# A memory-attention and FFT kernel: full-array products that may run as four 32-column tiles, a score unit of four groups, a new order

## The chip, the cores and the metric

The kernel runs on one core of a Trainium2 chip. The core's engines run side by side, each with an instruction queue of its own: TensorE (PE, matrix products into PSUM), VectorE (DVE), ScalarE (ACT), GpSimd (POOL), and SyncE (SP), which here only issues transfers. The metric is the device time of one execution in microseconds. The kernel before was timed three times: 245.85 us median, 242.32 lowest, 248.95 highest.

## The reference

Two branches over the same sequence length and width (2,048 tokens, 640 features) are mixed by a gate per token:

```python
x = A_x
g = sigmoid((x * gate_w).sum(-1, keepdims=True))
return g * A(x, wq, wk, wv, wo, beta) + (1 - g) * B(B_x, B_w_r, B_w_i)

def A(x, ...):                       # 32 heads of 20, 4 segments of 512 tokens
    for s in range(4):
        p = softmax(qs @ ks^T * scale + mask)      # causal inside the segment
        a_dot = p @ vs
        a_mem = (phi(qs) @ M) / (phi(qs) @ z + 1e-6)   # phi(t) = t + 1 if t > 0 else exp(t)
        o = sigmoid(beta) * a_mem + (1 - sigmoid(beta)) * a_dot
        M += phi(ks)^T @ vs;  z += sum(phi(ks))
    return o @ wo

def B(x, w_r, w_i):
    return irfft2(rfft2(x) * (w_r + 1j * w_i))
```

## The kernel before, in words

**The work.** Each of four segments has the projections of queries, keys and values (`proj_direct`, `proj_tile`, `v_part`), the feature map phi of queries and keys (in `proj_tile`: an exponential on ScalarE, a maximum and a minimum on VectorE, per tile of 128 rows by 512 tokens), the read of the memory built by earlier segments (`mem_read_tile`), the scores and their exponentials (`qk_unit`), causal masks on GpSimd (`mask`), the values (`pv_flipped` in segments 0 to 2, `pv_group` in segment 3), and the update of the memory (`mem_update`). The FFT branch (`fft`) is a chain of products with constant tables, named in the profile by their operands: `fcat,xsb` and `big,Ac` first, `Bt,tt` and `tt,Yt` in the middle, `big,Cp` last. `finish_tile` adds both branches and writes the result. Ten products on zeros (`warm_up`) run on TensorE while the first inputs are loaded.

**Shapes of TensorE.** `mms` (line 506) issues a group of products. It has a `mode`: 0 is the full array, weights of 128 rows by 128 columns; 1 is the score shape, weights of 20 rows by 64 columns, eight side by side; 2 is the split shape, weights of 128 rows by 32 columns, four side by side, each of which writes 32 PSUM partitions. A product with mode -1 may run full or, as four split products of 32 weight columns, in mode 2. Only the output projections of segments 0 to 2 (`finish_tile`, `oproj`, traced on line 520) have -1. The projections, the FFT, the memory's read and update and the gate's transposition have mode 0, and so have the value products of segment 3. Values of segments 0 to 2, the value projection of odd token tiles and the gated FFT products (`G,fbg`) have mode 2.

**Scores.** A head group is four heads; a segment has eight groups. `UNITS` (line 582) lists a pair's five score units: (first group, key blocks a), (first, b), (second, a), (both, last blocks c), (second, b). Each unit takes all four PSUM banks of the pool `qk`, then one exponential by ScalarE (two for b in the last segment) writes the tile `ex`. `ex` has three slots of 5,120 elements per partition, and group g uses slot g mod 3 (counted through all segments); a group's values are read from its slot before the third group behind it overwrites it.

**The order.** What runs when is no loop order. `record` lists all operations with what they read and write; `ORDER` (line 587) is a written list of 2,328 entries, each the number of an operation and which of its possible engines runs it. `Sched.schedule` walks the list with a model of costs (`HOPS`, `COST`, `QUEUE`) to place PSUM banks, semaphores and, for mode -1, the shape; `emit` writes each engine's instructions in that order with the waits that the reads and writes ask for. An engine carries out its instructions strictly in that order. All transfers but a few at the start and the end are on SP's queue.

For mode -1 the shape is chosen in `schedule`: a product that adds to a bank keeps the shape that the bank was begun in; one that begins a bank takes the shape of the product ahead of it; and behind a score unit it takes that of the next fixed work, or the full array where that is a score unit again.

**The gate.** The gate weight is the 641st column of `wv`; the value projection's second part has 321 columns and gives the gate's sums with it (`v_part`). In odd token tiles, whose rows are written in another order by split products, two exponentials of 64 rows bring them back; in even tiles it is one of 128 rows.

## Time and profile before

| | |
|---|---|
| median of three runs | 245.85 us |
| the profiled execution's own time | 246.08 us |
| its span, first to last instruction | 244.0 us |
| granted TensorE clock, mean | 0.993 |
| busy: TensorE / VectorE / ScalarE / GpSimd | 226.9 / 200.7 / 200.4 / 167.2 us |
| TensorE products / weight loads | 4,349 / 4,361 |
| transfers | 42.17 MB, 173 GB/s on average |

Busy time is the union of an engine's instructions as the profile draws them. Products of TensorE overlap in it: one of 320 columns is drawn about 300 ns long although the next can start some 136 ns later, so distances between starts say more than lengths. In the shape of a group, "128*32 128x320" means weights of 128 rows by 32 columns and a moving operand of 128 rows by 320 columns. Most products are issued by one line (L522 of `mms`; L520 for those that are split), so they are told apart by the names of their operands. A few records of products are missing in the trace.

### The profile page before, as it was taken

How to read it: one execution, taken by the hardware profiler on the slowest of the kernel's cores; microseconds unless marked ns; L12 is line 12 of the kernel's file. 1: busy time of each engine (PE TensorE's matmuls, PEld its weight loads, DVE VectorE, ACT ScalarE, POOL GpSimd, SP SyncE). 2: the span in 40 equal slices, each digit the busy share in tenths (PEclk: the TensorE clock that was granted, in tenths of full speed). 3: DMA queues.
4: the chain of work that ended last, by engine and by line, in shares of the span. 5: the costliest groups of instructions: out<-in, count | busy, mean ns of one | idle time of the engine just before them, and what ended most of it. 6: DMA issues, size and time to landing. Idle time of an engine off the chain costs nothing.

```text
span 244.0 us, 10261 instructions
## 1 busy us (share of the span) xinstructions
PE 226.9 (93%) x4349; PEld 140.8 (58%) x4361; DVE 200.7 (82%) x478; ACT 200.4 (82%) x243; POOL 167.2 (69%) x298
## 2 busy tenths in 40 slices
PE   7999999999979999899799979998999989999994
PEld 2674666766455665455575545565554546566793
DVE  0299989889999987999997998998999996735473
ACT  2388989988989999899898879999999968687801
POOL 8334069447959938649779895968898783857730
PEclk9999999999999999999999999999999999799999
DMA  7999959996977975849637583463876759382213
GB/s 168 301 330 268 209 173 182 233 194 199 214 209 131 189 222 147 183 141 252 159 98 203 134 247 97 126 169 105 227 172 201 182 130 206 95 87 83 72 67 108
DMA packets 58928, 42.17 MB, mean 173 GB/s; under 512 B 30020, under 2 KB 55172, under 8 KB 58884
## 3 DMA queue, kind: packets, MB, share of 16 engines
q1 hardware_dynamic: 57188, 40.71, 67.9%
q10 hardware_dynamic: 1696, 0.82, 1.2%
q8 instruction: 34, 0.56, 1.0%
q14 instruction: 10, 0.08, 0.1%
HBM read 23.32 MB, written 12.30 MB: 146 GB/s over the span
## 4 chain that ended last, share of the span: by engine, by line
PE 63%; DVE 16%; ACT 10%; DMA 7%; issue 2%; ACTq 0%; SPq 0%; DVEq 0%
PE psum L522 57%; ACT ex L1271 8%; PE psum L520 5%; DMA r<-r_scr 2%; DMA xT<-in_A_x_dram 2%; DVE Yt L1452 2%; DVE Pt L1447 2%; DVE phk L1093 2%; DMA dnc<-u_scr 2%; DVE oU L1534 1%; DMA u_scr<-ub 1%; ACT et L1080 1%; DVE Cp L533 1%; DVE ub L533 1%; DVE G L1493 1%
## 5 line engine op out<-in xcount | busy, mean ns | idle before, releaser
L1271 ACT ACTIVATE ex<-psum 128x2048 bf16<-128x2048 f32 (+4 forms) x92 | 138.6, 1506 | 15.5 <-PE psum L522 13.1
L1292 POOL TENSOR_SCALAR_AFFINE_SELECT ex<-ex 128x256 bf16<-128x256 bf16 (+2 forms) x224 | 122.6, 570 | 35.3 <-ACT ex L1271 32.8
L522 PE MATMUL psum<-qkp 20*64 20x64 bf16 (+5 forms) x1280 | 32.7, 271 | 3.9 <-ACT ex L1271 2.9
L522 PE MATMUL psum<-xT,wk 128*128 128x256 bf16 (+1 forms) x280 | 33.8, 281 | 0.6 <-DMA xT<-in_A_x_dram 0.4
L522 PE MATMUL psum<-wv,xT 128*32 128x320 bf16 (+3 forms) x400 | 29.4, 301 | 0.0
L522 PE MATMUL psum<-xT,wq 128*128 128x512 bf16 (+1 forms) x123 | 28.0, 385 | 0.8 <-issue 0.5
L1447 DVE TENSOR_TENSOR Pt<-psum,Wt 128x642 bf16<-128x642 f32 x32 | 25.5, 821 | 0.6 <-PE psum L522 0.2
L522 PEld LDWEIGHTS psum<-qkp 20*64 20x64 bf16 x1280 | 13.4, 103 | 21.6 <-ACT ex L1271 15.1
L522 PEld LDWEIGHTS psum<-xT,wk 128*128 128x128 bf16 (+1 forms) x280 | 19.8, 99 | 8.3 <-issue 1.8
L520 PE MATMUL psum<-wo,oU 128*32 128x320 bf16 x480 | 22.2, 305 | 0.5 <-DVE oU L1542 0.2
L522 PE MATMUL psum<-big,Ac 128*128 128x161 bf16 (+2 forms) x96 | 17.6, 257 | 2.0 <-DVE va L1123 1.5
L522 PE MATMUL psum<-ex,va 128*32 128x64 bf16 (+3 forms) x576 | 17.6, 257 | 1.8 <-DVE Pt L1447 1.3
L522 PE MATMUL psum<-big,Cp 128*128 128x321 bf16 (+1 forms) x96 | 18.1, 307 | 1.0 <-DVE G L1493 0.6
L522 PEld LDWEIGHTS psum<-wv,xT 128*32 128x32 bf16 (+1 forms) x400 | 14.5, 96 | 7.4 <-issue 2.0
L1123 DVE TENSOR_TENSOR va<-psum,ebx 128x320 bf16<-128x320 f32 x32 | 15.3, 483 | 2.9 <-PE psum L522 1.8
L914 POOL TENSOR_TENSOR xsb<-xf 128x320 bf16<-128x320 bf16 (+2 forms) x9 | 7.6, 846 | 14.4 <-DVE xsb L914 10.3
L522 PEld LDWEIGHTS psum<-ex,va 128*32 128x32 bf16 x576 | 11.0, 96 | 10.7 <-DVE Pt L1447 2.2
L1493 DVE TENSOR_TENSOR G<-eo,psum 128x320 bf16<-128x320 f32 x32 | 14.9, 478 | 2.3 <-PE psum L522 1.9
L533 DVE CAST ot<-psum 128x320 bf16<-128x320 f32 x18 | 8.5, 488 | 9.8 <-PE psum L520 7.9
L1080 ACT ACTIVATE et<-qu 128x512 bf16<-128x512 bf16 x25 | 15.3, 625 | 0.9 <-DVE phk L1093 0.9
L522 PE MATMUL psum<-tt,Yt 128*128 128x256 bf16 (+1 forms) x96 | 15.6, 274 | 0.3 <-DVE mem L1165 0.2
L1452 POOL TENSOR_TENSOR Yt<-Pt 128x321 bf16<-128x321 bf16 x17 | 12.7, 758 | 4.4 <-PE psum L522 3.9
(96 smaller groups left out, 401.2 us busy)
## 6 DMA issues: line engine op xcount, KB each, us to landing
qkp<-qk_scr SPq DMA_DIRECT2D x28, 160.0 KB
tt<-tab_tt SPq DMA_DIRECT2D x8, 512.0 KB, 4.3
qk_scr<-qu SPq DMA_DIRECT2D x12, 256.0 KB, 3.0
u_scr<-ub SPq DMA_DIRECT2D x12, 256.0 KB, 3.1
xsb<-in_A_x_dram SPq DMA_DIRECT2D x8, 320.0 KB, 4.9
oU<-u_scr SPq DMA_DIRECT2D x15, 128.0 KB, 3.2
out_dram<-ot SPq DMA_DIRECT2D x12, 160.0 KB
Wt<-in_B_w_r_dram SPq DMA_DIRECT2D x16, 80.2 KB, 3.2
```

The lines of the kernel that those rows point to most:

```text
L520: h = e.matmul(dst, wt, r_, start=st, stop=sp_, **{**kw, "tile_position": (0, q), "skip_group_check": True})
L522: h = e.matmul(o_, l_, r_, start=st, stop=sp_, **kw)
L533: alts["dve"] = (lambda e: e.tensor_copy(dst(), src()), 67 + 1.04 * n, 68.0)
L914: self.either(lambda e, dst=dst, src=src, d0=d0, n=n, op=op: e.tensor_tensor(xs.ap(o + dst, [D, 2], [1, n]), xf.ap(src + d0, [321, 2], [1, ...
L1080: self.one("act", lambda e: e.activation(et.ap(0, [1, L]), qsl(), ACT.Exp), L, [qb], [b("et", pi_)], late, name="phi_exp")
L1093: fmin = lambda e: e.tensor_tensor(dst(), dst(), et.ap(0, [1, L]), ALU.min)
L1123: self.one("dve", lambda e: e.tensor_tensor(va.ap(i * H * VW + h0 * VW, [VW, nh], [1, DH]), self.ps(bank, 0, [DH, nh], [1, DH]), self.ebx. ...
L1271: self.one("act", lambda e, d=d, q=q: e.activation(self.ex.ap(*d), self.ps(bank, *q), ACT.Exp, scale=SC), n, [bank], [self.exb(s, 2 * pr + ...
L1292: self.one("pool", lambda e: e.affine_select(self.ex.ap(e0 + d0, [1280, 4], [1, n], np_=np_), self.ex.ap(e0 + s0, [1280, 4], [1, n], np_=np_),
L1447: self.one("dve", lambda e, ri=ri, Pt=Pt, Wt=Wt, wo_=wo_, bank=bank: e.tensor_tensor(Pt.ap(ri * 322, [644, 2], [1, KD]), self.ps(bank, 0, ...
L1452: fn = lambda e, r=r, a0=a0, a1=a1, op=op, Pt=Pt, Yt=Yt: e.tensor_tensor(Yt.ap(r * 322, [1, KD]), Pt.ap(a0 * 322, [1, KD]), Pt.ap(a1 * 322 ...
L1493: self.one("dve", lambda e, q=q, n2=n2, bank=bank, eo=eo: e.tensor_tensor(self.G.ap(n2 * D + 639 * q, [1 - 2 * q, 320]), eo.ap(q, [1, 320] ...
```

## The change

- **Shapes.** Every full-array product but those of the last segment's values and the warm-up gets mode -1 in place of 0. Its cost in the planner is a pair, one for each shape.
- **Score units.** In segments 0 to 2 the units are listed per half segment (`HALF`): the last key blocks of four groups are one unit with one exponential of 2,048 elements per partition, behind the units a and b of groups 0, 1, 2 and ahead of the values of group 0; units a and b of group 3 follow, then the values of groups 1, 2 and 3. These blocks go to the tails of four slots (`hole`), so `ex` has four slots; the main part of a group still uses one of three. The rest of the fourth slot houses small tiles (`ub`, `Mz`, `dn`, gate tiles, `beta`).
- **Feature map.** The two tiles that are stored together get one exponential, one maximum and one minimum of 1,024 in place of two each of 512.
- **Memory read.** One reciprocal of 32 for both halves of a token tile in place of two of 16.
- **Gate.** Odd token tiles get their sums from products of one column (`odd_gates`, ten per segment) and one exponential per segment.
- **Planner and buffers.** The planner's costs are new (hops per engine, a price for a second wait, a fixed 95 for a change of shape, costs per transfer), tiles are packed to 32 bytes, `gT` shares a place with `dnr` and `rs` lies on the first columns of `fcat`. `ORDER` is a new list, with 2,264 entries.

The core of the diff (the list `ORDER`, most of the planner and the tile addresses are left out):

```diff
+def pe_cost(cols, mode):
+    if mode == 0:
+        return round(sum(max(n / 2.4 + 2.6, 25.2) for n in cols)), 178 if cols[-1] > 60 else 161
+    if mode == 2:
+        return round(sum(max(n / 9.6 + 1.0, 7.5) for n in cols)), 203 if cols[-1] > 64 else 213
+    return {12: (265, 239), 16: (261, 212), 24: (155, 269), 48: (300, 262)}[len(cols)]
...
-            self.mms(items, [b("w" + which + "a"), b("w" + which + "b"), xb[c], bank], [], prio, name="proj", mode=0)
+            self.mms(items, [b("w" + which + "a"), b("w" + which + "b"), xb[c], bank], [], prio, name="proj", mode=-1)
...
-                    self.mms(items, [b("xsb", 2 * nb + l2 // 2), b("fcat"), bank], [], prio, name="F1", mode=0)
+                    self.mms(items, [b("xsb", 2 * nb + l2 // 2), b("fcatF"), bank], [], prio, name="F1", mode=-1)
...
-                    self.mms([(th, n)], [b("Ac", c, nb) for nb in range(4)] + [b("big"), bank], [], prio, name="D", mode=0)
+                    self.mms([(th, n)], [b("Ac", c, nb) for nb in range(4)] + [b("big"), bank], [], prio, name="D", mode=-1)
...
+    HALF = (((0,), 0), ((0,), 1), ((1,), 0), ((1,), 1), ((2,), 0), ((2,), 1), ((0, 1, 2, 3), 2), (0, -1), ((3,), 0), ((3,), 1), (1, -1), (2, -1), (3, -1))
     UNITS = (((0,), 0), ((0,), 1), ((1,), 0), ((0, 1), 2), ((1,), 1))
...
     def attend(self, s):
         b = self.b
-        for pr in range(4):
+        if s < 3:
+            for half in range(2):
+                for u, (gps, kind) in enumerate(self.HALF):
+                    if kind < 0:
+                        self.pv_flipped(s, 4 * half + gps)
+                    else:
+                        self.qk_unit(s, 4 * half, u, (gps, kind))
+        for pr in range(4) if s == 3 else ():
             for u, parts in enumerate(self.UNITS):
-                self.qk_unit(s, pr, u, parts)
+                self.qk_unit(s, 2 * pr, u, parts)
...
-            outs = [((e0 + sh, [1280, 4], [step, 2], [1, 128]), (0, [512, 4], [128, 2], [1, 128]))]
+            outs = [((sh, [1280, 4], [5120, 4], [1, 128]), (0, [512, 4], [128, 4], [1, 128]))]
...
+        if t not in (1, 2, 4) or not ((which == "q" and s >= 1) or (which == "k" and s <= 2)):
+            return
+        m = 1 if t == 2 else 2
+        first, n_el = t + 1 - m, m * L
...
+        self.one("act", lambda e: e.activation(et.ap(0, [1, n_el]), qt.ap(po, [1, n_el]), ACT.Exp), n_el, rb, ebuf, late, name="phi_exp")
...
+        self.one("dve", lambda e: e.reciprocal(dn.ap(32, [1, 32]), dn.ap(0, [1, 32])), 32, [b("dn", k, q) for q in range(2)], [rb], prio, fix=145, name="mem_rec")
...
+    def odd_gates(self, s, prio, xT, xb):
+        self.Sc.group += 1
+        b = self.b
+        bank = Bank(1, "gen")
+        for i in (1, 3):
+            items = []
+            for c in range(5):
+                items.append((lambda i=i, c=c: (self.ps(bank, i // 2, [1, 1]), xT.ap(c * L + i * P, [1, P]), self.wv.ap(c * (D + 1) + D, [1, 1]),
+                                                c == 0, c == 4, {"skip_group_check": True}), 1))
+            self.mms(items, [b("gw"), bank] + xb, [], prio, name="gatep", mode=-1)
+        self.one("act", lambda e: e.activation(self.gr.ap(4 * s + 1, [2, 2]), self.ps(bank, 0, [1, 2]), ACT.Exp, scale=-1.0), 2,
+                 [bank], [b("gr", s, 1)], prio, name="gate_exp")
```

## The prediction

> **What bounds the kernel now.** First the page: the span, the busy shares and the chain that ended last.

> ```profile
> span 244.0 us, 10261 instructions
> ...
> PE 226.9 (93%) x4349; PEld 140.8 (58%) x4361; DVE 200.7 (82%) x478; ACT 200.4 (82%) x243; POOL 167.2 (69%) x298
> ...
> PE 63%; DVE 16%; ACT 10%; DMA 7%; issue 2%; ACTq 0%; SPq 0%; DVEq 0%
> ```

> The path runs on TensorE for 63% of the span; VectorE and ScalarE carry most of the rest. Next, busy time by stretch, since an average hides stages (columns: stretch, its length, then busy us and instructions of PE, weight loads, DVE, ACT, POOL; then clock, DMA share, GB/s).

> ```profile
> 0.00:50.00 50.00, 48.23 (x724) 30.04 (x726) 37.01 (x94) 36.90 (x56) 25.97 (x42) 1.00 0.94 236
> 50.00:195.00 145.00, 135.10 (x2418) 80.20 (x2425) 134.29 (x314) 134.10 (x152) 113.14 (x210) 1.00 0.69 174
> 195.00:235.00 40.00, 37.98 (x1071) 25.41 (x1060) 25.32 (x64) 28.53 (x35) 28.13 (x47) 0.96 0.54 112
> ```

> Up to 50 us and from 195 us TensorE is alone at the limit (48.2 of 50, 38.0 of 40). Between them three engines stand within a microsecond of each other: 135.1, 134.3 and 134.1 of 145 us. So in the long middle an edit that lightens one engine only hands the bound to the next; it has to lighten all three.

> "Busy" does not say how much of TensorE's time is products. The timeline of PE does (start, length, operation; the shape is weights rows*columns, then the moving operand; counts merge neighbours). The distance between two starts is the real price.

> ```profile
> 29.14 0.84 PE L522 MATMUL psum<-wv,xT 128*128 128x320 bf16 x5
> 29.82 0.38 PE L522 MATMUL psum<-xT,wq 128*128 128x512 bf16 x1
> ...
> 30.58 0.39 PE L522 MATMUL psum<-fcat,xsb 128*128 128x128 bf16 x4
> 30.80 0.38 PE L522 MATMUL psum<-xT,wq 128*128 128x512 bf16 x1
> ...
> 45.48 0.72 PE L522 MATMUL psum<-ex,va 128*32 128x512 bf16 x24
> 46.03 0.72 PE L522 MATMUL psum<-wv,xT 128*32 128x321 bf16 x16
> ...
> 86.31 0.60 PE L522 MATMUL psum<-xT,wk 128*128 128x256 bf16 x4
> 86.84 0.73 PE L522 MATMUL psum<-ex,va 128*32 128x512 bf16 x24
> 87.40 0.86 PE L522 MATMUL psum<-wv,xT 128*32 128x320 bf16 x20
> 88.19 0.42 PE L522 MATMUL psum<-qkp 20*64 20x320 bf16 x16
> ```

> Five full-array products of 320 columns take 29.82 - 29.14 = 0.68 us, 0.136 each; four of 128 columns take 0.22, 0.055 each. The 24 tile products at 45.48 are six pieces of 512, 384, 192 and three times 64 columns, four tiles side by side: 1,280 columns, which at the full-array pace would take 4 x 0.136 = 0.54; they take 0.55. So **a split product streams as fast as a full one**, and going from one kind of work to another in the same shape costs nothing (87.40 - 86.84 = 0.56 again). Where the shape changes there is a gap: four products of 256 columns are 0.435, yet 0.53 passes to 86.84; five split products of 320 are 0.68, yet 0.79 passes to 88.19. That is 0.095 to 0.11 us **per change of shape**.

> **The change part by part.** (1) Shapes. Following the starts through the whole timeline, full and split meet directly 58 times (31 into split, 27 into full); in 46 of them the gap is under 0.115 us, so nothing but the change of shape is there (4.53 us in total, 0.0985 each). First and last of the 46:

> ```profile
> 6.99 0.39 PE L522 MATMUL psum<-G 128*128 128x512 bf16 x1
> 7.30 0.40 PE L522 MATMUL psum<-xT,wk 128*32 128x256 bf16 x8
> ...
> 234.75 0.62 PE L522 MATMUL psum<-fcat,on 128*128 128x128 bf16 x8
> 235.30 0.91 PE L522 MATMUL psum<-wo,oTl 128*32 128x320 bf16 x20
> ```

> After the change a full product takes the shape of what ran before it, or, behind a score unit, of the next fixed work. What stays fixed in the full shape is the warm-up and the value products of the last segment, which make six of the 46 (the first one above and five from 194 us on). So 40 changes go, 40 x 0.0985 = -3.9 us (bounds 0, if the new order lets none go, and -5.7 for all 58). In the 12 others TensorE waits for data anyway; I take nothing.

> (2) Score units. In three of four segments the last key blocks of four head groups share one unit instead of two: six units fewer, each entered and left by a change of shape, 12 x 0.095 = -1.1 us. The streamed columns are the same.

> (3) The gate column of the odd token tiles moves into 40 full products of one column. The nearest row are the last segment's products of 21 columns:

> ```profile
> 222.89 1.17 PE L522 MATMUL psum<-va,ex 128*128 128x21 bf16 x40
> 223.98 0.43 PE L522 MATMUL psum<-qkp 20*64 20x512 bf16 x12
> ```

> 40 in 1.09 us less one change of shape: 0.025 each, so +1.0 us. TensorE: -3.9 - 1.1 + 1.0 = **-4.0 us**.

> (4) ScalarE (groups by shape: count, busy us, mean ns, idle before).

> ```profile
> L1271 ACT ACTIVATE ex<-psum 128x2048 bf16<-128x2048 f32 x56 | 105.1, 1877 | 7.2 <-PE psum L522 5.5
> L1080 ACT ACTIVATE et<-qu 128x512 bf16<-128x512 bf16 x25 | 15.3, 625 | 0.9 <-DVE phk L1093 0.9
> L1271 ACT ACTIVATE ex<-psum 128x1024 bf16<-128x1024 f32 x12 | 12.3, 1024 | 1.7 <-PE psum L522 1.4
> L1121 ACT ACTIVATE gate<-psum 64x1 f32<-64x1 f32 x16 | 2.6, 165 | 0.5
> ```

> Twelve exponentials of 1,024 become six of 2,048: 12.3 to 6 x 1.877 = 11.3, -1.0. Of 30 feature exponentials of 512 (the 25 here and five on the first segment's buffer), 24 become 12 of 1,024; that size from memory is not in the trace: between 1.024 (the score row of that size) and 2 x 0.625. I take the first: 24 x 0.625 - 12 x 1.024 = -2.7 (other end 0). Sixteen gate exponentials become four: -12 x 0.165 = -2.0. ScalarE: **-5.7 us** (-3.0).

> (5) VectorE.

> ```profile
> L1093 DVE TENSOR_TENSOR phk<-phk,et 128x512 bf16<-128x512 bf16 x15 | 9.8, 655 | 0.0
> L1163 DVE RECIPROCAL dn<-dn 128x16 f32<-128x16 f32 x24 | 5.5, 241 | 0.3
> L1160 DVE SCALAR_TENSOR_TENSOR dn<-psum,ebg 128x16 f32<-128x16 f32 x24 | 3.5, 152 | 0.1
> L1219 DVE RECIPROCAL dnr<-dnc 128x128 f32<-128x128 bf16 x3 | 2.8, 945 | 0.4 <-DMA dnc<-u_scr 0.4
> ```

> 24 feature maxima and 24 minima (655 ns is the longest group) become 12 and 12. What goes is 24 times the fixed part of an instruction, at most the 152 ns of one on 16 elements and at least nothing; the middle, 0.08, gives -1.9. The 24 reciprocals of 16 become 12 of 32: the slope between the two rows is (945 - 241) / 112 = 6.3 ns, so 342 each, 5.8 to 4.1, -1.7. VectorE: **-3.6 us** (-1.7 to -5.3).

> The joint reciprocal adds a wait: the first half's multiplication now stands behind the second half's products, some three of 154 columns at 0.065, and VectorE's whole in-order queue behind it, with the PSUM copies that TensorE waits for. That is 0.2 us twelve times, 2.4 at worst; I take nothing, since another VectorE instruction can stand in between. A joint feature exponential starts one PSUM copy later, and so does the transposing transfer of the key features on SP's queue (their number is the same); the products that read them come microseconds later, so nothing, or 0.6 us for each of six pairs on ScalarE if that cover is gone. GpSimd's masks and SP's transfers keep their number. The smaller buffers (a tile shared by two uses, a table's columns reused in the last segment) wait for work long done: nothing, or a few tenths per segment.

> So all three bounding engines lose nearly the same: 4.0, 5.7, 3.6. The least relieved sets the pace: I take **-3.7 us** on the span.

> (6) The order. It is new for every engine, and the trace cannot price it; bounds come from what an order can move: TensorE's idle time from 50 to 235 us, 9.9 + 2.0 = 11.9 us. At best it goes, at worst it doubles. I take a quarter off, -3.0, because waits behind exponentials and VectorE shrink with (4) and (5).

> Sum: 246.1 us (the profiled execution, span 244.0 and 2.1 around it) - 6.7 = 239.4. That execution lies 0.2 above the median 245.85, so from the median it is 239.1: **239 us**.

> **The rivals.** *The order gives more.* Half or more of the 11.9 us go beside the 3.7: 229 to 235, say 233. For it: three engines at 93% have slack that a search can pair. Against it: each such wait needs another engine free at that place.

> *Balance kept, waits back.* The work goes but the new order's waits take it back, or few shapes are unified because score units sit between: 241 to 250, say 244. For it: three engines bound together, so a gain needs all three at each place.

> *Slower: the four-group unit starves ScalarE.* There are still three slots for score tiles. The fourth group's exponential overwrites the first group's slot, so it waits for that group's values, which wait for the joint unit's masks.

> ```profile
> L1292 POOL TENSOR_SCALAR_AFFINE_SELECT ex<-ex 128x256 bf16<-128x256 bf16 x128 | 60.1, 480 | 29.7 <-ACT ex L1271 28.4
> L1292 POOL TENSOR_SCALAR_AFFINE_SELECT ex<-ex 64x512 bf16<-64x512 bf16 x64 | 43.4, 683 | 5.3 <-ACT ex L1271 4.4
> ```

> Masks 2 x 0.480 + 0.683, then the value products 0.73 (row at 86.84): 2.4 us without a score exponential, six times, 14 us. Behind the waiting instruction stands ScalarE's whole in-order queue, and behind that the PSUM copies TensorE needs. Before, the joint unit of two came with one more unit behind it as cover. Against it: of ScalarE's 200.4 us the rows of part 4 hold 117.4 of score exponentials, so up to 83 are other work (less by the last segment's smaller ones) that can be placed there. It decides when more than 11.6 of the 14 us stay unfilled (6.7 gained plus 4.9 for 2%); with all of it unfilled the time is 239 + 14 = 253.

> *Split products are starved of weights.* A split product needs four weight loads and four products. If each pair kept the 0.025 us of the row at 222.89, a split product could not be under 0.10 us. That touches 296 products of 88 to 176 columns, of which the largest and the smallest group are

> ```profile
> L522 PE MATMUL psum<-fcat,xsb 128*128 128x128 bf16 x80 | 8.9, 219 | 0.0
> L522 PE MATMUL psum<-va,pkn 128*128 128x176 bf16 x12 | 1.4, 240 | 0.0
> ```

> At 0.0375 to 0.075 us now (128 columns: 0.055) they would lose 0.04 on average: +12 if all were split, +6 for half; 251 or 245. Against it: at 45.48 the three 64-column pieces have 0.55 - 0.46 = 0.09 us, 0.03 for four pairs, though only in a short burst. [...]

> **How the numbers follow.** Forecast, 235 to 241: 0.43. Order gives more: 0.13. Waits back: 0.24. ScalarE starved: 0.14. Starved weights: 0.06, half of it slower by over 2%. Two per cent is about what a measurement can tell here (240.9 and 250.8). Faster 0.43 + 0.13 = 0.56; same 0.24 + 0.03 = 0.27; slower 0.14 + 0.03 = 0.17. The range 231 to 251 leaves out the best of the second case (0.03), the fourth (0.14) and a little of the fifth, about 0.19; it takes in the ends of parts 1, 4 and 5 (at 0, -3.0 and -1.7 with the order at nothing: 245).

> **What would show it.** Full and split meeting fewer than 20 times; 320 columns still 0.136 and 128-column products still 0.055 when split; 62 exponentials of 2,048 and 12 of 1,024 near 1.02; ScalarE near 195 and VectorE near 197 busy; TensorE's idle time near 9. ScalarE gaps of over 1 us before each half's fourth group would show the third rival; split short products 0.1 apart the fourth. A new order with its own waits of over 4 us in the middle makes the forecast wrong.

## The result and the profile after

The changed kernel takes 266.0 us (median; 265.3 to 271.7) against 246.1 of the kernel before beside it: ratio **1.092 [1.074, 1.109]**, slower. The forecast was 239, the range 231 to 251. The profiled execution is the longest, 271.73 us. Ratios compare executions without the slow ones, medians count all of them.

The page of the changed kernel, the lines that answer to those of before (TensorE's granted clock in 40 slices among them), and then two lines of before's page that were not shown yet:

```profile
span 270.0 us, 13454 instructions
...
PE 237.8 (88%) x5985; PEld 150.7 (56%) x5985; DVE 202.4 (75%) x440; ACT 194.2 (72%) x204; POOL 176.8 (65%) x309
...
PEclk9799999896799999999999999999895999979998
...
q8 instruction: 47, 0.77, 1.3%
...
PE 63%; DVE 18%; issue 8%; DMA 6%; ACT 2%; SPq 1%; DVEq 0%
```
```profile
PEclk9999999999999999999999999999999999799999
...
q8 instruction: 34, 0.56, 1.0%
```

ScalarE has come down as forecast, 200.4 to 194.2. But TensorE holds 5,985 products and as many weight loads in place of 4,349 and 4,361, the queue that brings instructions moves 47 packets in place of 34, the chain has 8% of "issue" (before 2%), and the clock is not full in eight slices (before in one). "Issue" is waiting that ends with no event the profile shows. The view of waits names the waiter, first in the changed kernel, then in the one before:

```profile
PE psum L552 <- issue: 8.7, 5, 3.9
PE psum L554 <- issue: 6.0, 4, 3.0
```
```profile
PE psum L522 <- issue: 1.6, 5, 0.6
...
PE psum L520 <- issue: 0.2, 1, 0.2
```

14.7 us in nine waits, the longest 3.9; before it was 1.8 in six, none over 0.6. The longest in TensorE's timeline, and then the stretches around it (columns as in the prediction: length, busy us of PE, weight loads, DVE, ACT, POOL, then clock, DMA share, GB/s):

```profile
40.46 1.00 PE L554 MATMUL psum<-wv,xT 128*32 128x320 bf16 x24
41.29 0.30 PE L552 MATMUL psum<-wv,xT 128*32 128x320 bf16 x1
45.44 0.32 PE L552 MATMUL psum<-wv,xT 128*32 128x320 bf16 x3 [3.85 <-issue]
```
```profile
41.20:45.50 4.30, 0.45 (x13) 0.11 (x9) 0.49 (x1) 0.46 (x1) 4.30 (x9) 1.00 1.30 142
46.30:49.70 3.40, 3.40 (x60) 1.91 (x58) 1.77 (x4) 3.37 (x3) 0.73 (x2) 0.50 0.32 67
49.70:53.00 3.30, 3.30 (x144) 2.70 (x132) 1.86 (x5) 1.44 (x4) 0.18 (x1) 1.00 0.90 217
```

TensorE stops **inside one product**: of four 32-column tiles with the same moving data, the first starts at 41.29 and the other three at 45.44. No operand can be missing there. Just before, 24 tile products (six full ones) take 41.29 - 40.46 = 0.83 us, 0.138 each, the full-array pace. During the stop the DMA engines are full (1.30), and a microsecond after it the clock is halved for 3.4 us: 60 products where the next stretch, nearly as long, has 144.

Counting TensorE's records from the start of the trace (products, weight loads and the 95 semaphore and drain instructions between them), this stop comes behind instruction 1,217, which is 4 x 256 + 193. All nine waits lie at the same remainder of 256. Each packet of the instruction queue has 16,384 bytes (34 of 34 before, 47 of 47 in the changed kernel), and 3,260 products and weight loads more than before come with 13 packets more, one packet for 251; 256 instructions in a packet would be of 64 bytes each. In all thirteen traces there are as many packets as 256 goes into TensorE's records, from 34 to 50 (before 8,807 / 256 = 34.4 and 34 packets, in the changed kernel 12,065 / 256 = 47.1 and 47). The starts of the packets follow TensorE's count: of the 81 packets of these two kernels 78 start 0.2 to 5.8 us after the count has passed one such place, three up to 0.3 us ahead of it, and each of the nine waits is at the next place. Five blocks of the changed kernel, then two of before (times in us, worked out from the packets' records and the count):

```
block passed at   packet landed   next place reached   TensorE goes on
after  33.1           36.2            35.5                  37.6
after  35.5           40.5            41.3                  45.4
after  53.9           56.4            56.6                  57.8
after  56.6           63.4            61.4                  64.6
after 148.8          151.9           152.0                 153.2
before 44.0           49.3            50.7                  50.7
before 50.6           54.9            59.4                  59.4
```

TensorE goes on 1.3 to 1.8 us after the landing in 25 of 29 stalls (those over 0.7 us of the changed kernel and four of the experiments), in the other four 2.8 to 5.0 us after it. The two longest stops are among these four. Of the one shown above the packet's record even ends 0.8 us before the place is reached, so a late landing is not what held it by the record; what did stays open. Before, a block lasts 7.1 us (median) and lands 2.5 us after the place was passed (mean), 5.3 at worst. After, it lasts 4.9 (median), in some split stretches 2.4 to 3.2, and lands after 2.9 (mean), at worst 6.9.

So the theory to test (**A, instruction feed**): a split product is eight instructions instead of two, and where a block is used up faster than the next one arrives TensorE stops; the half clock then adds its share. Rivals: (**B**) the split form itself is slow; (**C**) the new order is bad in itself.

### The profile page after: what moved, and what is told of

Same layout as the page of the kernel before. It is cut to its first block, busy times and chain, and to the rows that moved or that the text cites. A ratio compares the mean times of both kernels' runs of the same rounds, so it can differ in the third digit from the quotient of the medians.

```text
span 270.0 us, 13454 instructions
## 1 busy us (share of the span) xinstructions
PE 237.8 (88%) x5985; PEld 150.7 (56%) x5985; DVE 202.4 (75%) x440; ACT 194.2 (72%) x204; POOL 176.8 (65%) x309
## 4 chain that ended last, share of the span: by engine, by line
PE 63%; DVE 18%; issue 8%; DMA 6%; ACT 2%; SPq 1%; DVEq 0%
PE psum L554 37%; PE psum L552 26%; DMA qk_scr<-q 3%; DVE Pt L1517 3%; DVE G L1563 2%; DMA xT<-in_A_x_dram 2%; SPq L588 1%; ACT ex L1337 1%; DVE ub L565 1%; DVE Yt L1522 1%; DVE oU L1604 1%; DVE oU L1612 1%; DMA qkp<-qk_scr 1%; DVE Cp L565 1%; DVE mem L1217 1%
## 5 line engine op out<-in xcount | busy, mean ns | idle before, releaser
L1337 ACT ACTIVATE ex<-psum 128x2048 bf16<-128x2048 f32 (+3 forms) x86 | 137.4, 1598 | 24.8 <-PE psum L554 23.6
L554 PE MATMUL psum<-xT,wk 128*128 128x256 bf16 (+1 forms) x210 | 23.3, 295 | 3.1 <-issue 3.0
L554 PE MATMUL psum<-wv,xT 128*32 128x320 bf16 (+3 forms) x350 | 24.1, 301 | 0.0
L552 PE MATMUL psum<-wv,xT 128*32 128x320 bf16 (+2 forms) x360 | 17.2, 268 | 5.9 <-issue 5.8
L552 PE MATMUL psum<-big,Cp 128*32 128x321 bf16 (+1 forms) x336 | 19.4, 346 | 2.9 <-DVE ub L565 1.5
L554 PE MATMUL psum<-xT,wq 128*128 128x512 bf16 (+1 forms) x90 | 19.0, 446 | 2.1 <-DMA xT<-in_A_x_dram 2.1
L953 POOL TENSOR_TENSOR xsb<-xf 128x320 bf16<-128x320 bf16 (+1 forms) x16 | 12.2, 768 | 11.9 <-DVE xsb L953 11.5
L565 DVE CAST qu<-psum 128x512 bf16<-128x512 f32 x19 | 13.0, 682 | 6.7 <-PE psum L554 5.7
L563 ACT ACTIVATE Ac<-psum 128x512 bf16<-128x512 f32 x13 | 7.5, 596 | 12.3 <-PE psum L552 6.7
L552 PEld LDWEIGHTS psum<-wo,oU 128*32 128x32 bf16 x480 | 13.2, 101 | 5.5 <-issue 1.9
```

Source lines behind the costliest of these rows:

```text
L552: h = e.matmul(dst, wt, r_, start=st, stop=sp_, **{**kw, "tile_position": (0, q), "skip_group_check": True})
L554: h = e.matmul(o_, l_, r_, start=st, stop=sp_, **kw)
L563: alts["act"] = (lambda e: e.activation(dst(), src(), ACT.Copy), round(65 + 0.833 * n), 111)
L565: alts["dve"] = (lambda e: e.tensor_copy(dst(), src()), round(67 + 1.04 * n), 94)
L953: self.either(lambda e, dst=dst, src=src, d0=d0, n=n, op=op: e.tensor_tensor(xs.ap(o + dst, [D, 2], [1, n]), xf.ap(src + d0, [321, 2], [1, ...
L1337: self.one("act", lambda e, d=d, q=q: e.activation(self.ex.ap(*d), self.ps(bank, *q), ACT.Exp, scale=SC), n, [bank], dst, prio - self.QK_L ...
```

## The experiments

Kernels with such stalls scatter by 1.5 to 3.5%, and the granted clock differs between executions of one kernel (0.946 to 0.985 in the changed one); where a profile is quoted that matters, its own time is given.

**One part at a time.** The changed kernel with every free product full except the output projection's (one of twelve such lines, shortened):

```
-            self.mms(items, [b("w" + which + "a"), ...], [], prio, name="proj", mode=-1)
+            self.mms(items, [b("w" + which + "a"), ...], [], prio, name="proj", mode=0)
```

> The changed kernel with its order, its four-group units and its merged operations, but all products that it lets run either way (except the output projections, as before) run on the full array. Theory A (TensorE is starved of instructions: the changed kernel stalls for 15 us where the profile names no releaser, each time 193 instructions past a multiple of 256): TensorE's stream shrinks from about 12,000 to 8,800 instructions, so waits without a releaser fall from 14.7 us to under 3 us; the order then has 301 changes of shape instead of 163, which costs 138 x 0.095 = 13 us; 257 to 263 us. Theory B (the new order waits for other engines, and the shapes have no part in it): the waits stay and the changes of shape come on top, 275 to 280 us.

And the kernel before, its order and its merges untouched, with only the shapes freed (the same edit the other way):

> The kernel before, with its own order, units and operations, where only the shapes are made free by the rule of the changed kernel: 12,028 instructions on TensorE for products and weights instead of 8,722, and 180 changes of shape instead of 216 (-3.4 us). Theory A: waits without a releaser of 8 to 15 us appear at blocks of 256 instructions; 250 to 260 us. Theory B (and part 1 of the prediction): 241 to 243 us.

The first: 256.5 us, just under the 257 to 263 that theory A expected, ratio 1.036 [1.025, 1.046], with 0.5 us of issue waits in all, none over 0.2. It has 301 changes of shape against before's 216, since the order was made for free shapes: 85 x 0.0985 = 8.4 us, and 3.4 us more of half clock than before; together more than its 10.7 us. So this sum leaves nothing for C, and nothing for a gain of the order either; but it is a sum of prices, not a run of the order by itself. The second: 263.9 us, ratio **1.078 [1.067, 1.089]**, above the 250 to 260 that A expected and far from B's 241 to 243: freeing the shapes alone brings most of the loss. Its four executions lie apart, 257.0, 262.3, 265.5 and 265.7 us; the ratio fits the last three; by the shortest alone it would be 1.05. Its waits and its timeline (profiled execution 257.0 us):

```profile
PE psum L522 <- issue: 7.2, 7, 2.6
PE psum L520 <- issue: 4.2, 5, 1.9
```
```profile
43.07 0.28 PE L520 MATMUL psum<-fcat,xsb 128*32 128x128 bf16 x8
43.18 0.31 PE L520 MATMUL psum<-wv,xT 128*32 128x321 bf16 x4
...
43.43 0.85 PE L520 MATMUL psum<-wv,xT 128*32 128x321 bf16 x18
46.16 0.31 PE L520 MATMUL psum<-wv,xT 128*32 128x321 bf16 x2 [1.88 <-issue]
```

Two products of 128 columns, split, take 43.18 - 43.07 = 0.11 us, 0.055 each, as full ones did. Theory B as the prediction had it (at least 0.10 us a split product) is gone; then comes the stop, again inside a product.

**Where it costs.** The changed kernel with TensorE's first 238 operations (to 62 us) full:

```
+                if not modes and i < 238:
+                    modes = [0]
```

> The changed kernel, but the products of TensorE's first 238 operations (up to about 62 us) run on the full array; after that free as in the changed kernel. 11,300 instructions, 199 changes of shape (+3.4 us). Theory A: the waits of 10.7 us at 35 to 65 us vanish, those after stay (about 4 us); 252 to 257 us. Theory B: 264 to 268 us.

256.9 us, ratio 1.043 [1.033, 1.053], within A's 252 to 257, and 6.1 us of issue waits, of which 0.9 before 65 us (in the changed kernel 9.8): half of the loss lay in the first quarter of the time. With 36 more changes of shape (3.5 us) it is still 9 us shorter than the changed kernel.

**Number or form.** The deciding run keeps before's order and its full shapes, and only cuts the *moving* columns of large products (256 and more) into four pieces:

```
-                    h = e.matmul(o_, l_, r_, start=st, stop=sp_, **kw)
+                        cut = [i * n // 4 for i in range(5)]
+                        for a, z in zip(cut, cut[1:]):
...
+                            h = e.matmul(dst, l_, mv, start=st and a == 0, stop=sp_ and z == n, **{**kw, "skip_group_check": True})
```

> The kernel before with its order and its shapes; only each full-array product of 256 or more moving columns is cut into four products of a quarter of the columns, still on the whole array with the same weights. TensorE's products rise from 4,361 to 6,380, so its instructions from 8,722 to 12,760, about as many as in the split kernels, without one 32-column tile and without one other change of shape. If what costs is the number of TensorE's instructions: stalls of TensorE with no releaser, 1 to 4 us each and 7 to 15 us together, at the same place of each block of 256 instructions as before, and 255 to 265 us. If what costs is the 32-column form: no such stalls, and only the pieces' own price, some 670 products by 0.008 us = 5 us (a piece of 64 columns 0.029 us, four 0.117 against 0.109), so 246 to 252 us.

263.4 us, ratio **1.078 [1.065, 1.091]**, the ratio of the kernel with freed shapes, without one more split product than before. Its packets, its waits, and its longest stop (profiled execution 266.4 us):

```profile
q8 instruction: 50, 0.82, 1.3%
```
```profile
PE psum L540 <- issue: 7.4, 5, 2.0
PE psum L542 <- issue: 5.6, 3, 3.9
```
```profile
223.14 0.40 PE L542 MATMUL psum<-qkp 20*64 20x320 bf16 x10
227.48 0.38 PE L542 MATMUL psum<-qkp 20*64 20x192 bf16 x6 [3.94 <-issue]
```

13.0 us of issue waits; the six stops over 1.5 us from start to start are all at remainder 193 of 256, the longest in a score unit that the edit does not touch. More instructions are enough, without the split form. And the split form showed no price of its own (0.055 and 0.138 us above), so B is out.

**Rate, not number.** If only the rate matters, the same split is free where blocks last longer. The kernel before, free products split from TensorE's operation 240 to 859 (54 to 200 us), full outside:

```
+                if not modes and not 240 <= i < 860:
+                    modes = [0]
```

> The kernel before with its own order, free products split only in the middle (TensorE's operations 240 to 859, about 54 to 200 us) and full ahead of it and behind it: 436 products split, 10,618 TensorE instructions, 188 changes of shape (before 216). If the price comes only where a block of 256 instructions is used up faster than the next one lands: in the kernel split everywhere all five stalls lay outside this stretch, so no stall over 0.5 us here, 28 x 0.0985 = 2.8 us fewer changes of shape, and 241 to 246 us. If the split form or the number of instructions has a price of its own: 57% of the 18 us of the kernel split everywhere, about 255 us.

Ratio **1.002 [0.996, 1.008]**. It rests on executions of 243.3 to 246.9 us; six of the ten took 247.3 to 251.5, and the median of all, 248.0, is 1.4% above before's 244.7. That is 57% of the added instructions, and a loss between none and 1.4%, where a price for each would give 255 us. The profiled execution took 246.5:

```profile
PE 225.9 (92%) x5291; PEld 142.6 (58%) x5291; DVE 201.7 (83%) x478; ACT 199.9 (82%) x243; POOL 168.0 (69%) x298
```
```profile
PE psum L524 <- issue: 1.4, 1, 1.4
```
```profile
50.00:195.00 145.00, 135.73 (x3310) 81.78 (x3307) 132.98 (x311) 133.82 (x153) 112.45 (x211) 1.00 0.71 179
```

One stall of 1.4 us, at 209.7 us, behind the split stretch; from 59 us on, inside it, blocks last 3.7 us or more and land within 3.4. TensorE has 9 us of idle time in this stretch that could have hidden a loss, but the trace shows no stop there to hide. And no gain: 28 changes of shape fewer are 2.8 us of TensorE, in a stretch where VectorE and ScalarE are as busy as TensorE is.

**Why blocks come late.** While a packet waits over 2.5 us to start, the DMA engines are about 0.8 to 1.3 busy (means by kernel, all thirteen, of 2 to 12 packets each); while it waits 0.5 to 1.5 us, 0.42 to 0.71. That speaks for a queue behind data, but does not show it. The limit on data in flight, first in the changed kernel, then in the kernel before with freed shapes, and alone as the control:

```
-    WINDOW = 1600000
+    WINDOW = 600000
```

> The changed kernel with one number altered: at most 0.6 MB of transfers under way instead of 1.6 MB. Theory A with the backlog of data transfers as the reason why a block of instructions comes late: blocks land sooner (1.5 to 3 us from the crossing instead of up to 7), waits without a releaser fall under 6 us, and the time falls to 252 to 260 us unless later loads take it back. If the delay of a block has nothing to do with the kernel's own transfers: waits near 15 us, 264 us or more.

> The kernel before with its shapes freed everywhere (12,028 TensorE instructions, 263.9 us), and with the bytes that data transfers may have in flight limited to 0.6 MB in place of 1.6 MB. If the instruction blocks come late because they stand behind data transfers: landings over 3 us fall from 19 of 47 to 6 or fewer, stalls from 10.6 us to under 4, and 250 to 257 us. If the blocks are slow by themselves: stalls of 8 us or more and 261 to 266 us.

> The kernel before with only the limit of 0.6 MB in place of 1.6 MB, as the control for the run with split shapes and that limit. No stall of TensorE without a releaser in either theory; what the limit costs by later data: 244 to 249 us.

Changed kernel: 264.6 against 266.0 us (single executions from 259.7 to 268.4), a miss in time; though its issue waits fell from 14.7 to 9.9 us and landings over 3 us from 18 to 6. Freed shapes: 258.4 us, ratio 1.052 [1.046, 1.059] in place of 1.078, landings over 3 us from 19 to 11, and the issue waits from 11.4 to 5.0 us. All three fell short of what the theory expected (250 to 257 us, 6 or fewer, under 4 us):

```profile
PE psum L522 <- issue: 3.5, 3, 2.6
...
PE psum L520 <- issue: 1.5, 2, 0.9
```

The control takes 251.5 us, ratio 1.018 [1.009, 1.028], above the 244 to 249 expected: the limit has a price of its own. So with less data in flight fewer blocks land late and TensorE waits less, in both pairs of traces. What that is worth in time is not settled: the profiled executions with freed shapes took 257.0 us without the limit and 257.2 with it. Nor is it settled what keeps the other blocks late.

**What a stop costs.** Three waits are added to the kernel before, each on another engine's result some 3 us away; no instruction is added:

```
+        for x, y in ((955, 75), (238, 304), (2188, 1935)):
+            ops[x].preds.append(ops[y])
```

> The kernel before with three waits added on TensorE, each on another engine's result planned some 3.3 us later: at about 28 us (a projection behind a VectorE fold), 44 us (a value projection behind a GpSimd mask) and 214 us (an output projection behind a GpSimd mask). Nothing else is changed, no instruction is added. If a stall also costs the half clock that follows it: gaps of 2 to 4 us, a stretch of 3.4 us at a granted clock of 0.50 within 3 us behind at least two of them, and 244 + 9 + 3 to 5 = 253 to 258 us, less what later waits take in. If the half clock has another cause: no more stretches than before (one of 3.4 us), and at most 253 us.

257.9 us, ratio 1.052 [1.046, 1.058]. Its three added waits, and the stretches with each gap and behind it:

```profile
PE psum L522 <- POOL ex L1294: 3.4, 1, 3.4
PE psum L524 <- DVE xsb L916: 3.2, 1, 3.2
PE psum L524 <- POOL ex L1294: 2.7, 1, 2.7
```
```profile
24.90:28.30 3.40, 0.63 (x3) 0.10 (x1) 3.40 (x11) 2.27 (x2) 0.00 (x0) 1.00 1.24 244
28.30:31.70 3.40, 3.00 (x12) 1.59 (x13) 0.34 (x2) 0.01 (x1) 0.00 (x0) 0.50 0.96 129
45.60:48.80 3.20, 0.55 (x5) 0.19 (x3) 1.46 (x4) 0.87 (x2) 2.92 (x6) 0.99 0.93 288
48.80:52.20 3.40, 3.40 (x18) 2.21 (x19) 1.26 (x3) 1.29 (x3) 0.00 (x0) 0.50 0.86 219
223.40:226.30 2.90, 0.46 (x16) 0.11 (x4) 0.19 (x1) 1.37 (x1) 1.98 (x4) 0.99 0.70 54
226.30:233.10 6.80, 5.89 (x96) 3.16 (x100) 0.49 (x1) 2.89 (x4) 2.87 (x6) 0.50 0.13 25
```

9.3 us of waits, and behind each the clock at 0.50 for 3.4 or 6.8 us: 13.6 us at half rate, 6.8 lost where before lost 1.7. 9.3 + 5.1 = 14.4, of which 13 are found. These three stops were paid about one and a half times.

**Splitting only short runs** in the changed kernel, to keep few instructions and few changes of shape:

```
+                    modes = [2 if (a == 2 and z == 2 and n <= 12) or (a + z == 3 and n <= 8) else 0]
```

> The changed kernel, in which a free product is split only in short runs that lie beside fixed split work (up to 12 products between two split neighbours, up to 8 between a score unit and a split neighbour), and is full elsewhere: 10,314 TensorE instructions and 228 changes of shape, against 11,994 and 163 in the changed kernel and 8,802 and 301 in the changed kernel with full products. If the number of instructions and the changes of shape are the whole account: 256.5 - 73 x 0.0985 = 249.3 us and up to 4 us of instruction stalls, 249 to 253 us. If the new order itself is bad: 255 us or more. If the order's gain is real and was only covered: under 246 us.

263.9 us, ratio 1.080 [1.069, 1.092]: a miss by 11 us, and in the range (255 us or more) that was to show a bad order, theory C. Its trace gives another account, of one execution: issue waits of 6.8 us (5.9 of them at 36 to 60 us, where the fixed work is split too), and 8.5 us more lost to half clock than in the kernel with full products. 249.3 + 6.8 + 8.5 = 264.6 us; the profiled execution took 263.6. So C is not needed, but no run excludes it. Of the half clock, 17 us are on end:

```profile
188.40:195.20 6.80, 5.26 (x148) 2.86 (x140) 6.23 (x18) 5.59 (x7) 6.80 (x10) 1.00 0.84 174
195.20:212.30 17.10, 16.99 (x191) 7.20 (x195) 11.02 (x26) 9.33 (x9) 7.04 (x14) 0.50 0.35 99
```

It follows a stop of 1.3 us at 194.0; why it lasts five times 3.4 us although TensorE is then busy throughout stays open.

**The feature map's merge alone**, in the kernel before. Each joint instruction stands in before's order where the later of its inputs is ready, so the run tests merge and place together:

```
-            self.one("act", lambda e: e.activation(et.ap(0, [1, L]), qsl(), ACT.Exp), L, [qb], [b("et", pi_)],
+        self.one("act", lambda e: e.activation(et.ap(0, [1, n_el]), qt.ap(po, [1, n_el]), ACT.Exp), n_el, rb, ebuf, late, name="phi_exp")
```

> The kernel before with one part of the change alone: the feature exponentials, maxima and minima of two head groups in one instruction (24 of the 30 become 12), the order kept except that a joint instruction stands where the later of its two inputs is ready. TensorE's instructions and shapes stay as they were. If the prediction's parts 4 and 5 are sized right: ScalarE's busy time 2.7 us less (0 to 2.7), VectorE's 1.9 us less (0 to 3.6), and 243 to 246 us. If the longer wait for the second group's copy takes it back: 246 to 249 us.

248.9 us, ratio 1.022 [1.012, 1.032], in the range of the second theory (the longer wait takes it back), and neither engine is relieved (ScalarE 200.3, VectorE 200.9; before 200.4 and 200.7). ScalarE's timeline of before, then of this kernel:

```profile
63.46 1.14 ACT L1080 ACTIVATE et<-qu 128x512 bf16<-128x512 bf16 x2
64.50 1.87 ACT L1271 ACTIVATE ex<-psum 128x2048 bf16<-128x2048 f32 x1
```
```profile
66.27 1.05 ACT L1063 ACTIVATE et<-qu 128x1024 bf16<-128x1024 bf16 x1
67.22 1.87 ACT L1248 ACTIVATE ex<-psum 128x2048 bf16<-128x2048 f32 x1
```

Two exponentials of 512 take 64.50 - 63.46 = 1.04 us from start to start, the joint one 0.95: 0.09 saved, not 0.625 x 2 - 1.024 = 0.23.

## Why the prediction was wrong

**Its reading of the bound** held: TensorE alone at both ends, three engines in the middle. It fits that the run with splits only in the middle gained nothing from fewer changes of shape. The stops, though, were not only at the ends: 5.5 of their 14.7 us lie between 50 and 195 us.

**Part 1 (shapes)** failed, and with it the sign. The count was right: 53 changes of shape fewer (163 in place of 216, counted from the products' shapes), where 40 and 12 were forecast; full and split meet directly 17 times in the trace, where fewer than 20 was the sign. Right, too, was "a split product streams as fast as a full one". The failing step is the one that made the sum of changes of shape alone: some 530 products became four each, and the six instructions that each of them adds were costed at nothing. The rate at which TensorE takes instructions was in no row that the prediction read, though the page has the packets of the instruction queue. The rows that seemed to clear it, bursts of some dozen tile products, are shorter than a block. Where the prediction put nothing, the runs showed that TensorE stopped for 14.7 us at places 256 instructions apart, with half clock at the three longest stops, and that added instructions alone cost as much (ratio 1.078) as the freed shapes (1.078). The fourth rival, starved of weights at 0.06, had the right sign, a loss by splitting, and the wrong thing that starves; its bound of 0.10 us for a short split product was not met (0.055).

The size, by the two profiled executions, which are 25.7 us apart: 14.7 - 1.8 = 12.9 us more issue waits, and six stretches of 3.4 or 6.8 us at 0.50, 27.3 us in all, of which half is lost, 13.7 us against before's 1.7. That is 24.9. The 5.2 us that 53 fewer changes of shape should save are therefore not seen; what took them back is not shown. The other executions of the changed kernel are shorter by 3 to 6 us and have less half clock (a granted clock of 0.984 over 264 us is 4.2 us lost); their waits are not on record.

**Parts 2 and 3.** 62 exponentials of 2,048 are there, and the one-column products are 0.025 us from start to start, as taken. The starved ScalarE, at 0.14, did not come: 19.3 us of waiting stand at that line against 5.5 before, but every one of these waits ends with score products and none with a group's values. The longest, 3.2 us, comes directly behind TensorE's stop at 235 us; for the rest the link to the stops is argued, not shown.

**Part 4** was right in its total (6.2 us against 5.7) and wrong in its reason; **part 5** missed its sign. The changed kernel's groups:

```profile
L1337 ACT ACTIVATE ex<-psum 128x2048 bf16<-128x2048 f32 x62 | 116.3, 1875 | 20.0 <-PE psum L554 19.3
L1123 ACT ACTIVATE et<-qu 128x1024 bf16<-128x1024 bf16 x10 | 10.5, 1050 | 0.3 <-DVE phq L1131 0.3
L1214 DVE RECIPROCAL dn<-dn 128x32 f32<-128x32 f32 x12 | 4.2, 350 | 0.3
```

The joint exponential is 1.05 where 1.024 was taken, the joint reciprocal 0.350 where 0.342 was. But the mean of an instruction is not its price on a busy engine: neighbours overlap (1.05 us long, 0.95 from start to start in the run with this merge alone), as the prediction itself found for TensorE and then did not apply to ScalarE. By starts, 12 joint exponentials save 12 x 0.09 = 1.1 us, not 2.7. Instead nine copies out of PSUM went to VectorE: summed over their groups they fall from 95 to 86 on ScalarE, by some 3 us, and rise from 109 to 118 on VectorE, by some 4. That, and other work that the new order gives to another engine, outweighs what VectorE's merges save: it went up by 1.7 us instead of down by 3.6, although its reciprocals fell from 5.5 to 4.2.

**Part 6 (order).** The quarter of TensorE's idle time that it was to save cannot be seen: what the all-full kernel loses is covered by its added changes of shape and half clock. This is an account, not a run of the new order by itself.

## What to carry to other kernels

Before an edit that multiplies TensorE's instructions, divide: time in which it uses 256 of them, against the time a block takes to land under the data traffic of that stretch; here 7.1 us against 2.5 (before: the median block, the mean landing) and at least 3.7 against at most 3.4 were safe, and 2.4 to 3.2 against up to 6.9 was not. Place such edits where the engine waits anyway (here the middle, at a ratio of 1.002), and take the price of a merged instruction from the distance between starts, not from its duration. What pointed to the instruction feed here were waits that end with "issue", all nine of the changed kernel at remainder 193 of 256, the longest inside one operation.
